# Linear attention and two MLPs on one core: PSUM tiles by bank, and loads over 128 partitions

## The chip, the cores and the metric

The kernel runs on one core of one Trainium2 chip. The metric is the device time of one execution in microseconds, taken as the median of several runs. Beside them one execution was profiled; every row below comes from that one.

## What is computed

Three stages follow one another. For B = 4 batches, H = 8 heads, S = 576 positions and D = 64 the attention is linear (no softmax), with an RMS norm per head and position; the result, 2304 rows of 512, goes through two MLPs with 2048 hidden units.

```python
kv  = np.einsum('bhsd,bhse->bhde', k, v)
out = np.einsum('bhsd,bhde->bhse', q, kv)
x   = out / sqrt(mean(out * out, -1) + 1e-6) * g_norm
x   = x.transpose(0, 2, 1, 3).reshape(2304, 512)
h = x @ w_in;  g = maximum(h, 0) + log1p(exp(-abs(h)));  y = g @ w_out      # first MLP
h = y @ w_in2; g = maximum(0.01 * h, h);                 return g @ w_out2  # second MLP
```

## The kernel before, in words

**Order of work.** The kernel does not issue its instructions in the order in which it names them. Every step is registered with `op` (L41): a cost for each engine that could do it (PE is TensorE, D VectorE, A ScalarE, P GpSimd, S a DMA from SyncE's queue, N nothing), a function that issues it, and keys that it reads and writes. `Plan.run` (L73) then lays all of them out greedily by due time, as its own costs see it, and issues each on the engine that it chose. Keys for PSUM are banks, `("ps", 0)` to `("ps", 7)`: two steps on different banks are independent for the planner. The waits that end up in the program are made later, by the framework, from the tiles that each instruction touches.

**PSUM.** Eight banks of 512 words per partition are allocated as four tiles of two banks, `pw[0]` to `pw[3]`, and every later step takes a slice of one of them:

```python
pw = ring(psum, "pw", 4, [P, 1024])
ps = [t[:, c:c + 512] for t in pw for c in (0, 512)]
```

So banks 0 and 1 are one tile, as are 2 and 3, 4 and 5, 6 and 7.

**Attention.** 16 units, each two heads of one batch. `load` (L393) brings q, k and v of a unit in three DMAs of SyncE's queue, into rings of four buffers with 96 partitions: partition p holds positions 6p to 6p+5, so one run of memory is 6 x 64 words. `T` (L405) copies q together (L374, L372 or GpSimd's L376), transposes it in six pieces (L419), forms kv of both heads in twelve matmuls with 96 rows each (L426; each shows as two in the trace) and copies both out of `pw[0]` or `pw[1]`, the latter for the first ten units alone (`U_H`). `O` (L461) multiplies q by kv into `pw[2]` (L467), copies to `xy` and squares (L485 on ScalarE, L487 on VectorE or GpSimd). After four units `norm` (L491) and `X` (L538) make and apply the norms. `xy` holds x, transposed, for all 2304 columns; within a batch column r * 96 + p is position 6p + r.

**MLPs.** 24 blocks t (two MLPs by `NG` = 4 groups of 512 hidden units by `NTP` = 3 pairs of 384 tokens) with seven Strassen products each way. Each operand is split in a high and a low part, so a product is six matmuls. `product` (L810) adds x-side products into U (bank 0 or 1, alternating with s), V (bank 2) and W (bank 3); the matmul line is L820, or L910 for the first blocks in `plain` (L897). `after` (L1116) moves them on: L1139 copies U to W on ScalarE, L1127 copies V or U to SBUF, L1134 adds them on VectorE, L835 and L841 apply the activation. `parts` (L845: L849 on ScalarE, L854 on VectorE) splits the activated blocks. `second` (L1029) multiplies by the second weight, in `piece(i, j)` (L1053):

```python
bank = (6 if i in (1, 3, 5) else 4) + (j // 2 if tokens else j)
```

In the first MLP (L1082, `tokens` false) j is 0 and 1, six matmuls of 384 columns for each of two banks; i runs 0, 5, 1, 2, 3, 4, 6. In the second MLP (L1077) j is 0, 1, 2: six matmuls of 256 columns each, the first two in one bank, the third in the bank beside it. `to_y` reads the bank and adds it to `xy` (L699 on VectorE; L693 and L694 copy where nothing has been added before); L1093 copies a bank to the other pair. Pieces are interleaved with the products of the next block, seven products and ten or eleven pieces a step s.

**Around it.** x parts are kept in DRAM and brought back (L803), weights are loaded and decoded from 64-bit floats (L572 to L626) and split (L661, L665), rows of the result are stored by L1020, 128 columns of `xy` at a time, cut where the position runs of 96 columns end.

Of the kernel before, what the change touches and what calls it, by code (L numbers as in the profile page):

```python
# [133 lines left out]
def linear_attention_two_mlps(  # L134
# [39 lines left out]
    R6 = 6  # L174
    PQ = S // R6
# [168 lines left out]
    both = mstp.tile([P, 4, 8], F32, name="both")  # L344
    nc.gpsimd.memset(ones, 0.0)
# [35 lines left out]
    def from_psum(out, in_, n, bank, writes):  # L381


        def fn(e):
            if e == "A":
                nc.scalar.activation(out, in_, AF.Copy)
            else:
                nc.vector.tensor_copy(out, in_)

        return op({"A": t_a(n), "D": t_d(n)}, fn, [], [("ps", bank), *writes])  # L390


    def load(u):  # L393
        b, hp = u // NPAIR, u % NPAIR
        hs = slice(2 * hp, 2 * hp + 2)
        for nm, src in (("q", q), ("k", k), ("v", v)):
            def fn(e, nm=nm, src=src):
                nc.sync.dma_start(
                    out=lda[nm][u % NLD],
                    in_=src[b, hs].rearrange("h (p r) d -> p h r d", r=R6),  # L400
                )

            op({"S": 0.93}, fn, (), [(nm, u % NLD)])

    def T(u):  # L405
        i = u % 2
        copy_to(
            qp[i], lda["q"][u % NLD].rearrange("p h r d -> p r h d"), R6 * P,
            [("q", u % NLD)], [("qp", i)], "AD" if u == 0 else "ADP",
        )  # L410
        t = i if u < U_H else 0
        k0, k1 = ("ps", 2 * t), ("ps", 2 * t + 1)
        qc = pw[t][:, 32:32 + S]
        kv = pw[t][:, 32 + S:32 + S + D]
        ka, va = lda["k"][u % NLD], lda["v"][u % NLD]

        def f_t(e):
            for r in range(R6):
                nc.tensor.transpose(  # L419
                    qc[:, r * PQ:(r + 1) * PQ], qp[i][:, r, :, :], ident[0:PQ, 0:PQ]  # L420
                )

        def f_kv(e):
            for r in range(R6):
                for h in range(2):
                    nc.tensor.matmul(  # L426
                        kv[h * D:(h + 1) * D, :], ka[:, h, r, :], va[:, h, r, :],
                        start=(r == 0), stop=(r == R6 - 1), tile_position=(0, h * D),
                    )

        op({"PE": 0.5}, f_t, [("qp", i)], [k0, k1])
        op({"PE": 0.75}, f_kv, [("k", u % NLD), ("v", u % NLD)], [k1])
# [24 lines left out]
    o_, s_of = pw[2][:, 0:S], pw[2][:, S:S + HS]  # L457
# [3 lines left out]
    def O(u):  # L461
        b, hp, i = u // NPAIR, u % NPAIR, u % 2
        cols = slice(b * S, (b + 1) * S)

        def f_o(e):
            for c0, c1 in ((0, 512), (512, S)):
                nc.tensor.matmul(  # L467
                    o_[:, c0:c1], kvm[i], qt[i][:, c0:c1], start=True, stop=True
                )
# [21 lines left out]
    def norm(b):  # L491
        def f_s(e):
            for w in range(NB):
                for c in range(4):
                    nc.tensor.matmul(
                        s_of[32 * c:32 * (c + 1), :], ones[:, 6 - 2 * w:38 - 2 * w],
                        sq[w][:, c * HS:(c + 1) * HS], start=(w == 0), stop=(w == NB - 1),
                        tile_position=(0, 32 * c),
                    )

        sk, rk = [("ps", 5)], [("rs", b % 2)]
# [3 lines left out]
            lambda e: nc.scalar.activation(fa, s_of, AF.Ln, bias=eps_b, scale=2.0 ** -SHIFT / D),  # L505
# [32 lines left out]
    def X(u):  # L538
# [10 lines left out]
        op({"PE": 0.28}, f_b, [("rs", b % 2), ("pick",)], RK)  # L549
# [10 lines left out]
    def decode_w(F, which, a_reg):  # L560
# [22 lines left out]
        op({"S": (1.65, 1.4)[which]}, f_l, after_loads if (which, f) < (1, GF) and which else (), rk)  # L583
# [105 lines left out]
    def to_xy(dst, src, n, first, bank, xk):  # L689
        if first:  # L690
            op(
                {"D": t_d(n), "A": t_a(n)},
                lambda e: nc.vector.tensor_copy(dst, src) if e == "D"  # L693
                else nc.scalar.activation(dst, src, AF.Copy),  # L694
                [("ps", bank)], xk,
            )
        else:
            op(
                {"D": t_d(n)}, lambda e: nc.vector.tensor_tensor(dst, src, dst, ALU.add),  # L699
                [("ps", bank)] + xk, xk,  # L700
            )
# [195 lines left out]
    def plain(s, k_):  # L897
        c = block(0, s, k_)
        w_ = wst[s % 2]
        for m in range(2):  # L900
            o = ps[2 + m][:, :BN]
            for j in range(2):
# [3 lines left out]
                def fn(e, j=j, o=o, e_=e_, W_=W_, part_=part_):  # L906
                    for kk in range(2):
                        at = part_ * 256 + kk * P
                        for n, (a, b) in enumerate(((0, 0), (0, 1), (1, 0))):
                            nc.tensor.matmul(  # L910
                                o, W_[:, a, at:at + P], e_[:, b, kk, :],
# [117 lines left out]
    def second(t):  # L1029
# [9 lines left out]
        def to_y(i, bank, j0, j1):  # L1039
            a, k_ = S_TO[i]  # L1040
            c0 = (2 * tp + k_) * BN
            if tokens:
                c0, n = c0 + j0 * P, (j1 - j0) * P
                dst = xy[:, 2 * a:2 * a + 2, c0:c0 + n].rearrange("p a (j n) -> p j a n", n=P)
                src = ps[bank][:, (j0 % 2) * 256:(j0 % 2) * 256 + 2 * n]
                src = src.rearrange("p (j a n) -> p j a n", a=2, n=P)
                kcs, n = [2 * a, 2 * a + 1], 2 * n
            else:
                kcs, n = [2 * a + j0], BN
                dst, src = xy[:, kcs[0], c0:c0 + BN], ps[bank][:, :BN]  # L1050
            to_xy(dst, src, n, g % NG == 0 and i in ((5, 1, 2, 6) if pre else (0, 1, 2, 6)), bank, xyk(kcs, c0, n // len(kcs)))

        def piece(i, j):  # L1053
# [4 lines left out]
            y = ps[bank]  # L1058
# [4 lines left out]
            def fn(e):  # L1063
                if widens:
# [23 lines left out]
            if i == 0 and pre:  # L1088
                if not tokens or j:
# [3 lines left out]
                        lambda e: nc.scalar.activation(ps[bank + 2][:, :n], y[:, :n], AF.Copy),  # L1093
# [22 lines left out]
    def after(s, i):  # L1116

        cA, cB = (block(s // 2, s % 2, k_) for k_ in range(2))
        U, V, W = (ps[u_bank(s, x_)][:, :BN] for x_ in range(3))
# [5 lines left out]
        def copy(c, m, src, bank):  # L1125
            op(
                {"A": t_a(BN)}, lambda e: nc.scalar.activation(c[:, m, :], src, AF.Copy),  # L1127
# [3 lines left out]
        def plus(c, m, src, bank):  # L1131
            op(
                {"D": t_d(BN)},
                lambda e: nc.vector.tensor_tensor(c[:, m, :], src, c[:, m, :], ALU.add),  # L1134
# [3 lines left out]
        if i == 0:  # L1138
            op({"A": t_a(BN)}, lambda e: nc.scalar.activation(W, U, AF.Copy), bu, bw)  # L1139
# [9 lines left out]
        elif i == 5:  # L1149
            act(s, lambda: cA[:, 1, :], lambda: W, BN, bw, ck(cA, 1))  # L1150
        else:
            act(s, lambda: cA[:, 0, :], lambda: U, BN, bu, ck(cA, 0))
# [5 lines left out]
    def norm_done(e):  # L1158
# [5 lines left out]
        buf(p, "lf", F32)  # L1164

# [15 lines left out]
    def warm(e):  # L1181
        for _ in range(N_WARM):
            nc.tensor.transpose(ps[7][:, 0:P], ident, ident)
# [22 lines left out]
    for i in range(NU + 1):  # L1206
        if i in W1_AT:
# [4 lines left out]
            plan.AHEAD = Plan.AHEAD  # L1212
        if i < NU:
# [16 lines left out]
       + [(t, i) for t in "qkv" for i in range(NLD)])  # L1230
    op({"N": 0.0}, norm_done, (), granules("rc", "lf")
       + [("sq", i) for i in range(NB)] + [("rs", i) for i in range(2)]
# [105 lines left out]
```

## Time and profile before

| | us |
|---|---|
| three runs | 840.98, 846.70, 846.88 (median 846.7) |
| the profiled execution | 844.57 |
| its span, first to last instruction | 842.6 |
| outside the span | 2.0 |

The span is what the trace shows; the time of an execution adds what lies around it. The attention takes the first 80 us or so, the MLPs the rest. PE's busy time counts from a matmul's start to its modelled end, and successive matmuls overlap; so the time that a row of matmuls needs is read from start to start.

### The profile page before, as it was taken

Reading aid. Unit: us, or ns where it says so; the run is one execution under the profiler, and the core shown is the slowest. Engines: PE = TensorE matmul, PEld = TensorE weight load, DVE = VectorE, ACT = ScalarE, POOL = GpSimd, SP = SyncE. Lnnn points to the kernel's source line nnn. Section 1 sums busy time; section 2 is a strip of 40 time slices with the busy share of each in tenths; the row PEclk is TensorE's granted clock in tenths of the full one; section 3 lists DMA queues with packets and bytes.
Section 4 is the critical chain, followed back from the end, with each engine's and each line's share of the span. In section 5 each row is a group of like instructions: output and inputs, shape, how many; then the busy total and the mean of one; then the engine's idle time right before and its main releaser. Section 6 shows DMA issues by size and latency. Waiting matters only on the chain. (4 is left out here: it accounts for less than half of the span.)

```text
span 842.6 us, 13729 instructions
## 1 busy us (share of the span) xinstructions
PE 796.1 (94%) x5309; PEld 750.1 (89%) x5309; DVE 677.9 (80%) x1049; ACT 537.3 (64%) x883; POOL 17.7 (2%) x26
## 2 busy tenths in 40 slices
PE   7879899999999999899999999999999999999996
PEld 6668789999899999899988988999999999999996
DVE  3787899999788987885798998898789876876565
ACT  2667878878577775764577687686577555454441
POOL 2220000000000000000000000000000000000000
PEclk9999999999999999999999999999999999999999
DMA  9995467675864884763676959674874752662814
GB/s 254 267 262 194 194 231 275 235 279 201 322 243 150 288 300 152 267 240 129 232 279 227 342 195 405 249 284 142 324 239 170 292 210 102 214 223 92 286 39 112
DMA packets 71249, 192.52 MB, mean 228 GB/s; under 512 B 5520, under 2 KB 45456, under 8 KB 71184
## 3 DMA queue, kind: packets, MB, share of 16 engines
q1 hardware_dynamic: 69504, 190.86, 64.9%
q8 instruction: 41, 0.67, 0.3%
q10 hardware_dynamic: 1680, 0.79, 0.3%
q14 instruction: 24, 0.20, 0.1%
HBM read 152.31 MB, written 39.32 MB: 227 GB/s over the span
## 5 line engine op out<-in xcount | busy, mean ns | idle before, releaser
L820 PE MATMUL pw<-ra 128*128 128x384 f32 x1932 | 390.5, 337 | 9.0 <-ACT pw L1139 3.4
L820 PEld LDWEIGHTS pw<-ra 128*128 128x128 f32 x1932 | 331.3, 188 | 16.3 <-ACT pw L1139 6.5
L1077 PE MATMUL pw<-rb 128*128 128x256 f32 x1512 | 209.6, 285 | 9.6 <-DVE xy L699 6.9
L1077 PEld LDWEIGHTS pw<-rb 128*128 128x128 f32 x1512 | 195.3, 189 | 22.6 <-DVE xy L699 17.1
L1082 PE MATMUL pw<-rb 128*128 128x384 f32 x1008 | 206.5, 339 | 7.8 <-DVE xy L699 3.7
L1082 PEld LDWEIGHTS pw<-rb 128*128 128x128 f32 x1008 | 174.6, 188 | 19.0 <-DVE xy L699 10.6
L699 DVE TENSOR_TENSOR xy<-pw,xy 128x384 f32<-128x384 f32 (+2 forms) x247 | 134.1, 549 | 71.3 <-PE pw L1077 49.9
L849 ACT ACTIVATE rb<-mf 128x768 fp32r<-128x768 f32 x154 | 129.2, 845 | 76.1 <-PE pw L1077 41.0
L854 DVE TENSOR_TENSOR rb<-mf,rb 128x768 fp32r<-128x768 f32 x154 | 146.6, 952 | 23.5 <-ACT rb L849 23.0
L1127 ACT ACTIVATE mf<-pw 128x384 f32<-128x384 f32 x92 | 44.7, 488 | 33.8 <-PE pw L820 32.9
L934 DVE TENSOR_TENSOR mf<-mf 128x768 f32<-128x768 f32 x68 | 64.1, 952 | 2.8 <-ACT mf L835 2.2
L1134 DVE TENSOR_TENSOR mf<-pw,mf 128x384 f32<-128x384 f32 x92 | 50.7, 553 | 12.8 <-PE pw L820 10.1
L1139 ACT ACTIVATE pw<-pw 128x384 f32<-128x384 f32 x46 | 22.1, 481 | 25.7 <-PE pw L820 25.3
L835 ACT ACTIVATE mf<-mf 128x768 f32<-128x768 f32 x26 | 22.0, 845 | 19.1 <-DVE mf L1134 19.0
L1093 ACT ACTIVATE pw<-pw 128x384 f32<-128x384 f32 (+2 forms) x44 | 21.1, 479 | 16.2 <-PE pw L1077 9.0
L999 DVE TENSOR_TENSOR rb<-rc,rb 128x512 fp32r<-128x512 f32 x44 | 29.7, 683 | 0.3 <-ACT rb L996 0.3
L996 ACT ACTIVATE rb<-rc 128x512 fp32r<-128x512 f32 x44 | 27.3, 626 | 2.0 <-PE pw L1077 0.8
L841 ACT ACTIVATE mf<-mf 128x768 f32<-128x768 f32 x24 | 20.2, 841 | 8.3 <-DVE mf L1134 8.2
L694 ACT ACTIVATE xy<-pw 128x384 f32<-128x384 f32 (+2 forms) x40 | 18.9, 481 | 10.3 <-PE pw L1077 4.8
L841 ACT ACTIVATE mf<-pw 128x384 f32<-128x384 f32 x32 | 15.7, 491 | 11.6 <-PE pw L820 11.2
L835 ACT ACTIVATE mf<-pw 128x384 f32<-128x384 f32 x32 | 15.6, 488 | 11.4 <-PE pw L820 11.3
L467 PE MATMUL pw<-qt,kvm 128*128 128x512 f32 (+1 forms) x64 | 20.2, 439 | 1.8 <-DVE fm L518 1.7
(116 smaller groups left out, 701.7 us busy)
## 6 DMA issues: line engine op xcount, KB each, us to landing
ra<-xscr SPq DMA_DIRECT2D x131, 768.0 KB, 6.3
xscr<-ra SPq DMA_DIRECT2D x30, 768.0 KB, 4.7
mf<-in_moe_w_in_dram SPq DMA_DIRECT2D x18, 512.0 KB, 6.1
mf<-in_moe_w_out_dram SPq DMA_DIRECT2D x18, 512.0 KB, 5.2
lf<-in_moe_w_in_dram SPq DMA_DIRECT2D x14, 512.0 KB, 6.2
lf<-in_moe_w_out_dram SPq DMA_DIRECT2D x14, 512.0 KB, 4.8
xscr<-xy SPq DMA_DIRECT2D x8, 768.0 KB, 6.2
qa<-in_q_dram SPq DMA_DIRECT2D x16, 288.0 KB, 8.7
```

Source lines behind the costliest of these rows:

```text
L699: {"D": t_d(n)}, lambda e: nc.vector.tensor_tensor(dst, src, dst, ALU.add),
L820: nc.tensor.matmul(o, w_[:, a, c:c + P], e_[:, b, kk, :], start=(not on and which < 2 and kk == 0 and n == 0), stop=(kk == 1 and n == 2), ...
L835: {"A": t_a(n)}, lambda e: nc.scalar.activation(dst(), src(), AF.Softplus),
L841: lambda e: nc.scalar.activation(dst(), src(), AF.Prelu, alpha=0.01),
L849: {"A": t_a(n)}, lambda e: nc.scalar.activation(g[:, 0, :, :], c.ap, AF.Copy),
L854: lambda e: nc.vector.tensor_tensor(g[:, 1, :, :], c.ap, g[:, 0, :, :].bitcast(F32), ALU.subtract),
L934: lambda e: nc.vector.tensor_tensor(to.ap, x.ap, y.ap, ALU.subtract),
L999: lambda e: ENG[e].tensor_tensor(w_[:, 1], src(), w_[:, 0].bitcast(F32), ALU.subtract), sk + hk, lk,
L1077: nc.tensor.matmul(y[:, 256 * (j % 2):256 * (j % 2 + 1)], G_[:, a, m, js], w_[:, b, m, :], **flags)
L1082: nc.tensor.matmul(y[:, :BN], w_[:, a, m, js], G_[:, b, m, :], **flags)
L1127: {"A": t_a(BN)}, lambda e: nc.scalar.activation(c[:, m, :], src, AF.Copy),
L1134: lambda e: nc.vector.tensor_tensor(c[:, m, :], src, c[:, m, :], ALU.add),
```

## The change

- PSUM: the two-bank tiles stay while the attention runs, in two pools (`psa` with `pw[0]`, `pw[2]`, `pw[3]`; `psb` with `pw[1]`). Before unit 10 (of 0 to 15) `psb` is closed and banks 2 and 3 come back as two tiles of one bank; when the norms are done the other six do. All uses of `ps[...]` are evaluated at issue (`src()`, `out()`), as the tiles exist only then.
- q, k, v: partition p holds positions 4p to 4p+3 of the first 512, in 128 partitions, five buffers in place of four; the last 64 positions of all heads of a batch come in one DMA per tensor and batch, in 64 partitions (runs of 64 words), with the other 64 partitions set to zero. A unit's transposes are five of 128 columns, its kv ten matmuls with 128 rows.
- Squares go to ScalarE or VectorE; GpSimd keeps the copies of q.
- In batches 1 and 3 the last 64 positions come first among the columns of `xy`, so a store of 128 columns meets one run, or two of 64 between two batches.
- Some costs that the planner uses change (loads of q, k, v and of weights, transposes, kv, `X`).

```diff
-        rows = out[b * S:(b + 1) * S, :].rearrange("(p r) d -> r p d", r=R6)
-        runs += [(PQ, rows[r]) for r in range(R6)]
+        rows = out[b * S:b * S + 4 * P, :].rearrange("(p r) d -> r p d", r=4)
+        left = (RL, out[b * S + 4 * P:(b + 1) * S, :])
+        runs += [left] * (b % 2) + [(P, rows[r]) for r in range(4)] + [left] * (1 - b % 2)
...
-    psum = ctx.enter_context(tc.tile_pool(name="psum", bufs=1, space=PSUM))
-    pw = ring(psum, "pw", 4, [P, 1024])
-    ps = [t[:, c:c + 512] for t in pw for c in (0, 512)]
+    psa = tc.tile_pool(name="psa", bufs=1, space=PSUM, side="right")
+    psb = tc.tile_pool(name="psb", bufs=1, space=PSUM)
+    psap, psbp = psa.__enter__(), psb.__enter__()
+    pw = [(psbp if i == 1 else psap).tile([P, 1024], F32, name=f"pw{i}") for i in range(4)]
+    ps = [None] * 8
+
+    def banks(old, name, which, **kw):
+        old.__exit__(None, None, None)
+        p = ctx.enter_context(
+            tc.tile_pool(name=name, bufs=1, space=PSUM, reuse_waits="tile", **kw)
+        )
+        for i in which:
+            ps[i] = p.tile([P, 512], F32, name=f"ps{i}")
...
-    NLD = 4
+    NLD = 5
-    lda = {nm: ring(attp, nm + "a", NLD, [PQ, 2, R6, D]) for nm in "qkv"}
-    qp = ring(attp, "qp", 2, [PQ, R6, 2, D])
+    lda = {nm: ring(attp, nm + "a", NLD, [P, 2, 4, D]) for nm in "qkv"}
+    ldr = {nm: ring(attp, nm + "r", 2, [P, H, D]) for nm in "qkv"}
+    qp = ring(attp, "qp", 2, [P, 4, 2, D])
+    for t, e_ in enumerate((nc.vector, nc.gpsimd)):
+        for n in "qkv":
+            e_.memset(ldr[n][t][RL:], 0.0)
...
-                    in_=src[b, hs].rearrange("h (p r) d -> p h r d", r=R6),
+                    in_=src[b, hs, 0:4 * P, :].rearrange("h (p r) d -> p h r d", r=4),
+        if hp == 0:
+            for nm, src in (("q", q), ("k", k), ("v", v)):
+                def fn(e, nm=nm, src=src):
+                    nc.sync.dma_start(
+                        out=ldr[nm][b % 2][:RL], in_=src[b, :, 4 * P:S, :].rearrange("h p d -> p h d")
+                    )
...
-            for r in range(R6):
-                nc.tensor.transpose(
-                    qc[:, r * PQ:(r + 1) * PQ], qp[i][:, r, :, :], ident[0:PQ, 0:PQ]
-                )
+            for r in range(4):
+                nc.tensor.transpose(qc[:, r * P:(r + 1) * P], qp[i][:, r, :, :], ident)
+
+        def f_tl(e):
+            nc.tensor.transpose(pw[t][:, 4 * P:5 * P], ql[:, h2, :], ident)
...
-            for r in range(R6):
+            for r in range(5):
...
-        op({"A": t_a(S), "D": t_d(S), "P": t_p(S)}, f_s, xk, [("sq", u % NB)])
+        op({"A": t_a(S), "D": t_d(S), }, f_s, xk, [("sq", u % NB)])
...
+        banks(psa, "psc", (0, 1, 4, 5, 6, 7), side="right")
...
+        if i == U_H:
+            op({"N": 0.0}, lambda e: banks(psb, "psd", (2, 3)), (), [("ps", 2), ("ps", 3)])
```

## Rows read from the trace of the kernel before

**Rows 1.** The page's first part: busy time, share of the span, instructions.

```profile
PE 796.1 (94%) x5309; PEld 750.1 (89%) x5309; DVE 677.9 (80%) x1049; ACT 537.3 (64%) x883; POOL 17.7 (2%) x26
```

**Rows 2.** Busy time by stretch; last three columns: granted clock, DMA share, GB/s.

```profile
10.00:30.00 20.00, 15.97 (x227) 11.65 (x226) 9.28 (x21) 9.07 (x18) 2.57 (x4) 1.00 1.09 271
30.00:50.00 20.00, 15.96 (x199) 12.13 (x198) 15.76 (x28) 13.74 (x27) 6.58 (x7) 1.00 1.09 262
...
200.00:300.00 100.00, 96.76 (x545) 93.65 (x544) 87.47 (x138) 69.24 (x112) 0.00 (x0) 1.00 0.65 234
300.00:400.00 100.00, 97.19 (x543) 93.28 (x541) 77.74 (x119) 59.96 (x96) 0.00 (x0) 1.00 0.60 219
400.00:500.00 100.00, 95.91 (x564) 91.34 (x564) 89.43 (x129) 71.36 (x116) 0.00 (x0) 1.00 0.71 253
...
700.00:800.00 100.00, 97.62 (x672) 93.56 (x671) 69.43 (x106) 48.75 (x78) 0.00 (x0) 1.00 0.53 182
```

**Rows 3.** PE's matmuls from 92 us on: busy us, mean ns, idle before.

```profile
L820 PE MATMUL pw<-ra 128*128 128x384 f32 x1932 | 390.5, 337 | 9.0 <-ACT pw L1139 3.4 <-DVE mf L1134 1.8 <-ACT mf L835 1.4
L1077 PE MATMUL pw<-rb 128*128 128x256 f32 x1512 | 209.6, 285 | 9.6 <-DVE xy L699 6.9 <-ACT xy L694 1.4 <-ACT pw L1093 0.3
L1082 PE MATMUL pw<-rb 128*128 128x384 f32 x1008 | 206.5, 339 | 7.8 <-DVE xy L699 3.7 <-ACT xy L694 1.9 <-DVE xy L693 1.1
L910 PE MATMUL pw<-ra 128*128 128x384 f32 x9 | 1.9, 334 | 0.0
```

**Rows 4.** The chain that ended last: start, us, what.

```profile
596.06 1.44 PE pw L1077 x12
597.49 1.04 PE pw L820 x6
```

**Rows 5.** Waits of PE's weight loads from 92 us: total, times, longest.

```profile
PEld pw L1077 <- DVE xy L699: 17.1, 31, 1.1
PEld pw L1082 <- DVE xy L699: 10.6, 24, 1.7
PEld pw L820 <- ACT pw L1139: 6.5, 11, 1.1
...
PEld pw L1082 <- DVE rb L854: 1.4, 2, 1.1
...
PEld pw L1082 <- ACT pw L1093: 0.2, 1, 0.2
```

**Rows 6.** Timeline in the first MLP: start, us, engine, what, [idle before].

```profile
302.19 1.20 PE L1082 MATMUL pw<-rb 128*128 128x384 f32 x6
...
304.10 0.55 DVE L699 TENSOR_TENSOR xy<-pw,xy 128x384 f32<-128x384 f32 x1
...
304.70 1.01 PEld L1082 LDWEIGHTS pw<-rb 128*128 128x128 f32 x6 [0.59 <-DVE xy L699]
304.70 1.33 PE L1082 MATMUL pw<-rb 128*128 128x384 f32 x6 [0.27 <-DVE xy L699]
```

**Rows 7.** Timeline in the second MLP and at its end.

```profile
810.95 0.68 DVE L699 TENSOR_TENSOR xy<-pw,xy 128x512 f32<-128x512 f32 x1
...
811.68 1.69 PE L1077 MATMUL pw<-rb 128*128 128x256 f32 x12
...
837.30 0.98 PE L1077 MATMUL pw<-rb 128*128 128x256 f32 x6 [0.52 <-DVE xy L699]
```

**Rows 8.** DMA traffic from 10 to 60 us, in 40 slices.

```profile
GB/s 281 277 278 278 286 280 273 263 279 252 253 265 261 277 243 284 242 275 275 278 270 272 274 263 280 250 259 262 244 272 238 235 270 268 270 269 272 275 272 263
```

**Rows 9.** DMA traffic from 300 to 400 us, in 40 slices.

```profile
GB/s 101 402 339 334 418 414 417 386 30 0 7 0 29 329 270 317 282 397 417 406 179 8 202 0 3 37 320 253 320 380 424 433 245 7 0 0 0 42 337 283
```

**Rows 10.** Groups of instructions of the attention, first 80 us.

```profile
L426 PE MATMUL pw<-va,ka 96*64 96x64 f32 x384 | 14.7, 225 | 6.5 <-DMA va<-in_v_dram 6.5
...
L419 PE MATMUL pw<-ident,qp 96*128 96x96 f32 x96 | 11.1, 252 | 3.6 <-POOL qp L376 3.1 <-DVE qp L374 0.3 <-ACT qp L372 0.3
...
L487 POOL TENSOR_TENSOR sq<-xy 128x576 f32<-128x576 f32 x5 | 6.0, 1193 | 8.5 <-DVE xy L477 6.3 <-ACT xy L475 2.2
```

More of the change, by code (lines that the diff above doesn't have):

```diff
@@ L173, in linear_attention_two_mlps @@
     NF = DFF // P
-    R6 = 6
-    PQ = S // R6
+    RL = S - 4 * P
     NPAIR = H // 2
@@ L399, in fn @@
                     out=lda[nm][u % NLD],
-                    in_=src[b, hs].rearrange("h (p r) d -> p h r d", r=R6),
+                    in_=src[b, hs, 0:4 * P, :].rearrange("h (p r) d -> p h r d", r=4),
                 )
-            op({"S": 0.93}, fn, (), [(nm, u % NLD)])
+            first = "qkv".index(nm) - 60.0 if u == 0 else None
+            op({"S": 0.74}, fn, (), [(nm, u % NLD)], due=first)
+        if hp == 0:
[4 more added lines that the diff above has]
+                    )
+                op({"S": 0.6}, fn, (), [(nm + "r", b % 2)])
     def T(u):
-        i = u % 2
+        b, hp, i = u // NPAIR, u % NPAIR, u % 2
+        h2 = slice(2 * hp, 2 * hp + 2)
         copy_to(
-            qp[i], lda["q"][u % NLD].rearrange("p h r d -> p r h d"), R6 * P,
+            qp[i], lda["q"][u % NLD].rearrange("p h r d -> p r h d"), 4 * P,
             [("q", u % NLD)], [("qp", i)], "AD" if u == 0 else "ADP",
@@ L455, in T, with o_of, s_of @@
         op({"A": t_a(S), "D": t_d(S)}, f_c, [], [k0, k1, ("qt", i)])
-    o_, s_of = pw[2][:, 0:S], pw[2][:, S:S + HS]
+    def o_of(b):
+        return pw[2][:, 4 * P - RL:] if b % 2 else pw[2][:, 0:S]
+    def s_of(b):
+        return pw[2][:, 0:HS] if b % 2 else pw[2][:, S:S + HS]
     r_ = pw[3][:, 512 - 2 * HS:512 - 2 * HS + S]
@@ L463, in O @@
         cols = slice(b * S, (b + 1) * S)
+        o_ = o_of(b)
         def f_o(e):
[L466 to L469, printed above, removed]
+            at = b % 2 * RL
+            nc.tensor.matmul(
+                o_[:, at:at + 4 * P], kvm[i], qt[i][:, 0:4 * P], start=True, stop=True
+            )
+            at = (1 - b % 2) * 4 * P
+            nc.tensor.matmul(
+                o_[:, at:at + RL], kvm[i], qt[i][:, 4 * P:S], start=True, stop=True
+            )
         op({"PE": 0.98}, f_o, [("kvm", i), ("qt", i)], OK)
@@ L495, in f_s @@
                     nc.tensor.matmul(
-                        s_of[32 * c:32 * (c + 1), :], ones[:, 6 - 2 * w:38 - 2 * w],
+                        s_[32 * c:32 * (c + 1), :], ones[:, 6 - 2 * w:38 - 2 * w],
                         sq[w][:, c * HS:(c + 1) * HS], start=(w == 0), stop=(w == NB - 1),
@@ L581, in decode_w @@
         rk, ak = r.keys(), a_reg.keys()
-        op({"S": (1.65, 1.4)[which]}, f_l, after_loads if (which, f) < (1, GF) and which else (), rk)
+        op({"S": (1.47, 1.3)[which]}, f_l, after_loads if (which, f) < (1, GF) and which else (), rk)
         op(
@@ L900, in plain, with o @@
         for m in range(2):
-            o = ps[2 + m][:, :BN]
+            def o(m=m):
+                return ps[2 + m][:, :BN]
             for j in range(2):
@@ L1044, in to_y, with src @@
                 dst = xy[:, 2 * a:2 * a + 2, c0:c0 + n].rearrange("p a (j n) -> p j a n", n=P)
-                src = ps[bank][:, (j0 % 2) * 256:(j0 % 2) * 256 + 2 * n]
-                src = src.rearrange("p (j a n) -> p j a n", a=2, n=P)
+                def src():
+                    y = ps[bank][:, (j0 % 2) * 256:(j0 % 2) * 256 + (j1 - j0) * 256]
+                    return y.rearrange("p (j a n) -> p j a n", a=2, n=P)
                 kcs, n = [2 * a, 2 * a + 1], 2 * n
@@ L1049, in to_y @@
                 kcs, n = [2 * a + j0], BN
-                dst, src = xy[:, kcs[0], c0:c0 + BN], ps[bank][:, :BN]
+                dst, src = xy[:, kcs[0], c0:c0 + BN], lambda: ps[bank][:, :BN]
             to_xy(dst, src, n, g % NG == 0 and i in ((5, 1, 2, 6) if pre else (0, 1, 2, 6)), bank, xyk(kcs, c0, n // len(kcs)))
@@ L1063, in fn @@
             def fn(e):
+                y = ps[bank]
                 if widens:
@@ L1092, in piece @@
                         {"A": t_a(n)},
-                        lambda e: nc.scalar.activation(ps[bank + 2][:, :n], y[:, :n], AF.Copy),
+                        lambda e: nc.scalar.activation(
+                            ps[bank + 2][:, :n], ps[bank][:, :n], AF.Copy
+                        ),
                         [("ps", bank)], [("ps", bank + 2)],
@@ L1118, in after @@
         cA, cB = (block(s // 2, s % 2, k_) for k_ in range(2))
-        U, V, W = (ps[u_bank(s, x_)][:, :BN] for x_ in range(3))
+        U, V, W = (lambda x_=x_: ps[u_bank(s, x_)][:, :BN] for x_ in range(3))
         bu, bv, bw = ([("ps", u_bank(s, x_))] for x_ in range(3))
@@ L1149, in after @@
         elif i == 5:
[L1150 removed]
+            act(s, lambda: cA[:, 1, :], W, BN, bw, ck(cA, 1))
         else:
[L1152 removed]
+            act(s, lambda: cA[:, 0, :], U, BN, bu, ck(cA, 0))
     def attention_done(e):
@@ L1229, in linear_attention_two_mlps @@
        + [(t, i) for t in ("qp", "qt", "kvm") for i in range(2)]
-       + [(t, i) for t in "qkv" for i in range(NLD)])
+       + [(t, i) for t in "qkv" for i in range(NLD)]
+       + [(t + "r", i) for t in "qkv" for i in range(2)])
     op({"N": 0.0}, norm_done, (), granules("rc", "lf")
+       + [("ps", i) for i in (0, 1, 4, 5, 6, 7)]
        + [("sq", i) for i in range(NB)] + [("rs", i) for i in range(2)]
```

49 lines of the change are left out of this document (28 added, 21 removed).

## The prediction

> **What bounds the kernel now.** I read the page's busy shares first. PE is busy 796.1 of 842.6 us and VectorE 677.9; GpSimd does next to nothing [rows 1]. So the question is where PE idles. The stretches show two regimes [rows 2]. From 10 to 30 us, PE is busy 15.97 of 20 us and the DMA engines are at 1.09 of their share, with 271 GB/s: the attention is fed by saturated queues. From 200 us on PE has 96 to 98 of 100 us, DMA 0.53 to 0.71, and VectorE between 69.4 (700 to 800) and 89.4 us (400 to 500). [...]
>
> Busy time flatters PE, since matmuls overlap. From start to start, six matmuls of 384 columns take 1.04 us and twelve of 256 take 1.44 [rows 4], that is 173.3 and 120 ns each. From 92 us on there are 1932 + 1008 + 9 of the first kind and 1512 of the second [rows 3]: 511.2 + 181.4 = 692.6 us. The last group starts at 837.30 and lasts 0.98 [rows 7], so the MLP stage takes 838.3 - 92 = 746.3 us. **53.7 us of it are not matmuls.**
>
> How much of that is waiting? PE's rows give 9.0 + 9.6 + 7.8 = 26.4 us of idle time [rows 3], the weight loads' rows 55.0 us in all (18 rows, the largest two, two others and the last shown) [rows 5]. One stall shows how these relate [rows 6]: the group at 302.19 and the product after it need 2 x 1.04 us, so the next group was due at 304.27 and came at 304.70. It lost 0.43 us, where PE's row says 0.27 and the weight loads' row 0.59: the mean of both. By the mean of both sums, waits cost 41 us; the other 13 us are 3 ns or so per matmul.
>
> Nearly all those waits are for an instruction that reads or writes PSUM: L699, L1139 and the like; the clear exceptions, such as L854, have 1.4 us and less a row [rows 5].
>
> **What those waits are for.** In the first MLP two L1082 groups in a row are j = 0 and j = 1, in different banks by the code. The L699 at 304.10 reads what the group of 302.19 wrote; it ends at 304.65, and the next group, for the bank beside it, starts 0.05 us later [rows 6]. It had no business with that bank. In the second MLP the twelve matmuls at 811.68 begin with j = 2, whose bank is not the one that a 512-word read (j = 0 and 1) takes; they start 0.05 us after that read's end at 811.63 [rows 7]. L820's wait for L1139 is the same: a copy into W (bank 3) holds up a product into V (bank 2). So I read the waits as made per tile, and the tile has two banks. The planner, whose keys are banks, had put the next group there because it thought it free.
>
> **The change part by part.**
>
> *One-bank tiles in the MLPs.* What ends later once the neighbour's wait is gone? PE's next piece needs its own bank, last read one group further back; with a product between, that is 0.72 + 1.04 to 2 x 1.04 us of grace, as much as the longest wait of the main rows (1.7) [rows 5]. [...] VectorE has 10.6 us to spare in 400 to 500 and 12.5 in 200 to 300 [rows 2], more than PE's some 5.5 us of stalls per 100 us (41 / 7.46), so it is no bound by itself, but a dense stretch can still be late. Of 41 us, 2.7 are waits on data that stay (L854's and three smaller rows of that answer); of the 38 left I count on 24, near two thirds. The ends: a third (13) if late reads only move the stall by a group, 36 if almost everything goes. Allocating the tiles costs no instruction. The hand-over waits for the last reader of the old tile, which the banks' keys asked for before.
>
> *Loads of q, k, v.* Before: 16 x 3 x 294,912 bytes = 14.16 MB, at the 270 GB/s of the stretch from 10 to 60 us [rows 8] 52.4 us of queue time. After: 12.58 MB in runs of 1024 bytes over 128 partitions, and 12 DMAs with 6144 runs of 256 bytes, 1.57 MB. Neither form stands in the trace alone. Traffic of whole 128-partition tiles reaches 402 to 433 GB/s at its best and 270 to 330 in the slices around 337 us [rows 9], so the main part lies between 12.58 / 0.414 = 30.4 and, at today's rate, 46.6 us; I take 300 GB/s, the lower group, as the runs get shorter than now: 41.9. The remainders lie between 3.8 us (414 GB/s) and 34.9 us, if a run of 256 bytes holds an engine as long as one of 1536 does now (1536 x 16 / 270 GB/s = 91 ns; 6144 x 91 / 16). I take half of today's rate, 11.6 us, nearer the lower end as bytes shrink six-fold. Sum 53.5 against 52.4: +1 us, with ends at -18 and +29. The twelve extra issues on SyncE's queue come where the queue waits on the engines anyway.
>
> [...]
>
> *PE's share of the attention.* The kv matmuls go from 24 records a unit to 20: 14.7 us x 4 / 24 = 2.4 us less [rows 10]. Transposes go from six of 96 columns to five of 128 (576 to 640 columns): 11.1 us busy before, between 9 and 12 after; I take no change. Little of the 2.4 counts while the queues lead; after 70 us no kv matmul is left to save on. I take -2 with the shorter copies of q (512 words a unit in place of 768).
>
> *Squares off GpSimd.* Five of 1.19 us [rows 10] become five of some 0.7 us on ScalarE or VectorE, both under half busy at 10 to 30 us and at 0.69 and 0.79 at 30 to 50 [rows 2]: hidden; uncovered they would be 3.6 us. Memsets of the zero halves lie under the first loads.
>
> *Stores.* 20 pieces in place of 36, under matmuls but for the last ones; nothing, at most 0.5 us at the end.
>
> **Sum.** Against the profiled execution, 844.6 us (2.0 outside the span): -24 + 1 - 2 = -25, so **820 us**. The median of the runs, 846.7, lies 2 us above the profiled execution; the range takes that in.
>
> **The rivals.**
>
> *VectorE is late next.* PE's stalls move from "the neighbour's read" to "my own bank's read". For it: 87 to 89 us of 100 busy in two stretches. Against: 69.4 and 77.7 in two others, and the waits are short against the grace. The gain is the lower end, 13, with -1 from the attention less 2 for the extra squares: 834.
>
> *The remainders hold the queues* (the slower side). Each 256-byte run costs an engine what a long run costs, 91 ns, and the attention, bound by its queues, grows by 29 us: 844.6 - 24 - 2 + 29 = 848. It ends above today from 83 ns a run on. For it: the queues are saturated from 10 to 60 us [rows 8], so nothing hides it. Against: a sixth of the bytes.
>
> *The loads get fast.* 128 partitions bring the rate of the other tiles, 414 GB/s, and the remainders half of it, 7.6 us: 38 in place of 52.4. PE then takes over as the attention's bound (it idles 4 of 20 us at 10 to 30 [rows 2]), so at most 10 us count: 844.6 - 24 - 10 = 810. [...]
>
> *The change does not do it.* The waits are not per tile: PE waits for VectorE's place in its queue, and the neighbour's read is only the last thing passed. Then the stage keeps its 746 us and the time is 844. Against: the 0.05 us after the neighbour's read, in both MLPs [rows 6, 7].
>
> **How the numbers follow.** 820 has 0.64, with 806 to 832 as its own range; VectorE late, 834, has 0.13; fast loads, 810, 0.10; no effect, 844, 0.07; slow remainders, 848, 0.06. The range that holds 8 in 10 goes from 804 (24 to 30 saved in the MLPs and 10 in the attention) to 837. A measurement tells about 1% from no change, 8.4 us. Faster by more: 820 and 810 whole, most of 834, together 0.84; within: the rest of 834, no effect and half of the slow remainders, 0.12; slower 0.04.
>
> **What would show it.** Right: PE's weight loads' waits for L699 and L1139 fall from 17.1 + 10.6 + 6.5 us to a third or less; the groups of L1082 follow each other at 1.04 us though the read of the group before is still running; the stage from the first L820 to the last L1077 falls from 746 to about 722 us; the first L820 still comes at 90 to 92 us. Wrong: the waits stay with the same names, or the same time turns up as L699 waiting while VectorE is full; or the first L820 comes at 100 us and later with 4 us waits for q, and the DMA share stays over 1 beyond 70 us.

## The result, and the profile after

The changed kernel takes 782.13 us (median of four runs, 781.27 to 782.43), the kernel before 845.62 beside it (840.98 to 846.88): a ratio of 0.926, with a 95% interval from 0.922 to 0.929. The prediction of 820 us had the right sign, and both the time and its range (804 to 837) were too high: 63 us went where 25 were counted.

First the page of the profile after, its first part, which answers to [rows 1]; then the stretches, which answer to [rows 2] (last three columns: granted clock, DMA share, GB/s).

```profile
PE 767.9 (98%) x5229; PEld 751.8 (96%) x5229; DVE 677.3 (87%) x1050; ACT 536.3 (69%) x888; POOL 13.0 (2%) x26
```

```profile
10.00:30.00 20.00, 17.99 (x216) 12.56 (x212) 9.39 (x22) 11.40 (x22) 2.12 (x3) 1.00 1.04 315
30.00:50.00 20.00, 17.90 (x190) 13.13 (x190) 18.21 (x32) 17.65 (x34) 4.04 (x5) 1.00 1.07 312
200.00:300.00 100.00, 100.00 (x578) 100.00 (x578) 88.44 (x140) 70.91 (x117) 0.00 (x0) 1.00 0.71 265
300.00:400.00 100.00, 100.00 (x579) 100.00 (x578) 84.43 (x130) 62.39 (x100) 0.00 (x0) 1.00 0.60 216
400.00:500.00 100.00, 99.81 (x659) 99.41 (x658) 95.95 (x142) 82.23 (x137) 0.00 (x0) 1.00 0.88 334
```

PE has no idle time left from 200 to 400 us, and 0.2 us of it in the densest stretch, 400 to 500 us, where VectorE is at 95.95 of 100. VectorE does the same work as before (677.3 and 677.9 us) in a shorter span. In the attention the queues are still full from 10 to 50 us (DMA share, the mean busy share of the 16 DMA engines, is over 1), but they move 315 and 312 GB/s instead of 271 and 262.

PE's groups from the first product on, by the new line numbers (L864 is the old L820, L1126 the old L1077, L1131 the old L1082), answer to [rows 3]; the two waits of the weight loads that are long enough to be listed from 80 us on answer to [rows 5].

```profile
L864 PE MATMUL ps<-ra 128*128 128x384 f32 x1932 | 386.4, 335 | 0.2 <-DMA ra<-xscr 0.2
L1126 PE MATMUL ps<-rb 128*128 128x256 f32 x1512 | 204.1, 282 | 0.0
L1131 PE MATMUL ps<-rb 128*128 128x384 f32 x1008 | 201.5, 334 | 0.2 <-DVE rb L898 0.2
```

```profile
PEld ps L1131 <- DVE rb L898: 0.5, 1, 0.5
PEld ps L864 <- ACT ps L1142: 0.5, 1, 0.5
```

Not one wait for a reader of the neighbouring bank is left, where two lines alone had 17.1 and 10.6 us: the first is for data (`rb`), and for the second PE's own row of L864, above, names a reload of x parts (`ra<-xscr`); the named L1142 had ended 0.5 us before. Matmul groups now follow each other at 1.04 us. The last line is the read, by ScalarE, of the bank that the group of 85.97 wrote (j = 0). It starts after the group of 88.05 has begun in the bank beside it (j = 1), which no longer waits for it:

```profile
84.93 1.20 PE L864 MATMUL ps<-ra 128*128 128x384 f32 x6
85.97 1.20 PE L1131 MATMUL ps<-rb 128*128 128x384 f32 x6
87.01 1.20 PE L864 MATMUL ps<-ra 128*128 128x384 f32 x6
88.05 1.20 PE L1131 MATMUL ps<-rb 128*128 128x384 f32 x6
...
88.19 0.47 ACT L738 ACTIVATE xy<-ps 128x384 f32<-128x384 f32 x1
```

Where the 62.5 us of span went, by the starts and ends of PE's groups in the two traces:

| us | before | after | difference |
|---|---|---|---|
| span's start to first product | 92.33 | 84.93 | -7.40 |
| first product to last matmul of the MLPs | 745.95 | 691.76 | -54.19 |
| last matmul to span's end | 4.3 | 3.4 | -0.9 |

One microsecond stands in the wrong line: before, six matmuls of the first blocks came behind the first product (6 x 0.173 us); after, all 96 come ahead of it. So the MLP stage gave 53.2 us and the attention 8.4. The stage after is its matmuls summed as in the prediction, 2940 x 0.1733 + 1512 x 0.12 = 691.0 us, plus 0.7.

### The profile page after: what moved, and what is told of

Read it like the earlier page. It is cut to its first block, busy times and chain, and to the rows that moved or that the text cites. A ratio compares the mean times of both kernels' runs of the same rounds, so it can differ in the third digit from the quotient of the medians.

```text
span 780.1 us, 13522 instructions
## 1 busy us (share of the span) xinstructions
PE 767.9 (98%) x5229; PEld 751.8 (96%) x5229; DVE 677.3 (87%) x1050; ACT 536.3 (69%) x888; POOL 13.0 (2%) x26
## 4 chain that ended last, share of the span: by engine, by line
PE 90%; DVE 5%; DMA 2%; SPq 1%; ACT 1%; issue 1%; POOL 0%; DVEq 0%; ACTq 0%
PE ps L864 41%; PE ps L1126 23%; PE ps L1131 21%; PE pw L505 1%; DMA qa<-in_q_dram 1%; PE pw L454 1%; DMA va<-in_v_dram 1%; DMA ra<-xscr 1%; PE ps L956 1%; DVE ra L766 1%; DVE rb L898 1%; SPq L412 1%; DVE rb L1045 1%; PE pw L588 1%; PE pw L443 1%
## 5 line engine op out<-in xcount | busy, mean ns | idle before, releaser
L864 PE MATMUL ps<-ra 128*128 128x384 f32 x1932 | 386.4, 335 | 0.2 <-DMA ra<-xscr 0.2
L864 PEld LDWEIGHTS ps<-ra 128*128 128x128 f32 x1932 | 331.9, 188 | 0.6 <-ACT ps L1142 0.5
L1126 PE MATMUL ps<-rb 128*128 128x256 f32 x1512 | 204.1, 282 | 0.0
L1131 PE MATMUL ps<-rb 128*128 128x384 f32 x1008 | 201.5, 334 | 0.2 <-DVE rb L898 0.2
L1126 PEld LDWEIGHTS ps<-rb 128*128 128x128 f32 x1512 | 198.2, 189 | 0.1
L1131 PEld LDWEIGHTS ps<-rb 128*128 128x128 f32 x1008 | 177.0, 188 | 0.5 <-DVE rb L898 0.5
L898 DVE TENSOR_TENSOR rb<-mf,rb 128x768 fp32r<-128x768 f32 x154 | 146.6, 952 | 23.8 <-ACT rb L893 22.5
L743 DVE TENSOR_TENSOR xy<-ps,xy 128x384 f32<-128x384 f32 (+2 forms) x247 | 134.6, 548 | 33.3 <-PE ps L1126 21.8
L1178 ACT ACTIVATE mf<-ps 128x384 f32<-128x384 f32 x92 | 44.6, 487 | 27.2 <-PE ps L864 26.4
L1185 DVE TENSOR_TENSOR mf<-ps,mf 128x384 f32<-128x384 f32 x92 | 50.6, 553 | 10.9 <-PE ps L864 9.4
L1190 ACT ACTIVATE ps<-ps 128x384 f32<-128x384 f32 x46 | 22.0, 479 | 24.6 <-PE ps L864 24.1
L879 ACT ACTIVATE mf<-mf 128x768 f32<-128x768 f32 x26 | 21.9, 843 | 15.1 <-DVE mf L1185 14.9
L1142 ACT ACTIVATE ps<-ps 128x384 f32<-128x384 f32 (+2 forms) x44 | 21.1, 481 | 7.2 <-PE ps L1131 3.7
L885 ACT ACTIVATE mf<-ps 128x384 f32<-128x384 f32 x32 | 15.7, 489 | 9.1 <-PE ps L864 8.9
L738 ACT ACTIVATE xy<-ps 128x384 f32<-128x384 f32 (+2 forms) x37 | 17.7, 484 | 5.7 <-PE ps L1126 2.7
```

The source lines that it names most:

```text
L743: {"D": t_d(n)}, lambda e: nc.vector.tensor_tensor(dst, src(), dst, ALU.add),
L864: nc.tensor.matmul(o, w_[:, a, c:c + P], e_[:, b, kk, :], start=(not on and which < 2 and kk == 0 and n == 0), stop=(kk == 1 and n == 2), ...
L885: lambda e: nc.scalar.activation(dst(), src(), AF.Prelu, alpha=0.01),
L898: lambda e: nc.vector.tensor_tensor(g[:, 1, :, :], c.ap, g[:, 0, :, :].bitcast(F32), ALU.subtract),
L1126: nc.tensor.matmul(y[:, 256 * (j % 2):256 * (j % 2 + 1)], G_[:, a, m, js], w_[:, b, m, :], **flags)
L1131: nc.tensor.matmul(y[:, :BN], w_[:, a, m, js], G_[:, b, m, :], **flags)
```

## The experiments

Two theories stood against each other at the start. A: the whole gain is the waits for the neighbouring bank, and the loads and the rest are small. B: another part of the change, or the new order of steps that the planner finds with it, freed PE. Each kernel was compared with the kernel before on the same chip.

**The kernel before with one-bank tiles alone.** The kernel before, with the change's PSUM allocation and nothing else (shown is the allocation; the uses of `ps[...]` are evaluated at issue, as in the change):

```
-    pw = ring(psum, "pw", 4, [P, 1024])
-    ps = [t[:, c:c + 512] for t in pw for c in (0, 512)]
+    pw = [(psbp if i == 1 else psap).tile([P, 1024], F32, name=f"pw{i}") for i in range(4)]
+    ps = [None] * 8
...
+            ps[i] = p.tile([P, 512], F32, name=f"ps{i}")
```

> The kernel before with one-bank PSUM tiles in the MLPs and nothing else of the change. Theory A (waits made for a two-bank tile cost the whole 53 us that the MLP stage lost): the stage takes some 692 us, the time is 844.6 - 53 - 1 = 790 us (786 to 794), and the first L820 still comes at 92 us. Rival B (the stage is free of stalls because the planner, with the new loads and costs, puts the steps in another order): the stage keeps some 745 us and the time stays at 835 to 845 us.

It took 790.44 us against 842.70, a ratio of 0.939 (0.936 to 0.941): 52 of the 63 us. The MLP stage went from 745.95 to 695.32 us. The first product came at 86.05 us, sooner than the 92 expected: the first blocks' waits in the attention went too (shown with the pairs below), and its loads, though unchanged, ran at 286 GB/s from 10 to 60 us where the first profile of before has 267. All waits of its weight loads that are listed from the first product (86.05 us) on, with times and the longest, and then PE's own row of the products:

```profile
PEld ps L1097 <- DVE rb L864: 1.6, 2, 1.1
PEld ps L830 <- DVE ra L732: 1.2, 1, 1.2
PEld ps L830 <- ACT mf L1144: 0.8, 1, 0.8
```

```profile
L830 PE MATMUL ps<-ra 128*128 128x384 f32 x1932 | 386.5, 335 | 1.5 <-DVE ra L732 0.9 <-DMA ra<-xscr 0.6
```

The first two are waits for data (`rb`, `ra`), as the prediction had them stay. The third is put down to L1144, which had ended 0.5 us before; PE's own row has a reload of x parts (`ra<-xscr`) in its place. None is for a reader of PSUM's neighbour.

**The change with two-bank tiles kept.** The changed kernel, allocating its banks in pairs in the MLPs too:

```
-            ps[i] = p.tile([P, 512], F32, name=f"ps{i}")
+            if i // 2 in (0, 1, 2, 3):
+                if i % 2 == 0:
+                    w = p.tile([P, 1024], F32, name=f"pd{i}")
+                    ps[i], ps[i + 1] = w[:, 0:512], w[:, 512:1024]
+            else:
+                ps[i] = p.tile([P, 512], F32, name=f"ps{i}")
```

> The kernel after, but the six and two banks come back as tiles of two banks each, sliced as before; the order of the steps is that of the kernel after. Theory A: the stalls of the MLP stage return, 782 + 53 = 835 us (831 to 838), and only the 8 us by which the first product came earlier remain. Rival B: the time stays at 782 to 788 us.

833.69 us, ratio 0.990 (0.988 to 0.992). The planner's keys are banks in either form, so the order of the work is that of the changed kernel; the waits are back, in nearly the old amounts (waits of its weight loads from the first product on; L1131, L1136 and L869 are the second MLP, the first, and the product):

```profile
PEld pd L1131 <- DVE xy L748: 17.1, 30, 1.5
PEld pd L1136 <- DVE xy L748: 10.6, 25, 1.7
PEld pd L869 <- ACT pd L1195: 6.4, 9, 1.2
```

So theory A holds in the main: the granularity of the tile is worth 52 us by either route, and the rest of the change 9 (842.70 less 833.69). In the profiles, 50.6 and 47.6 us of it lie in the MLP stage.

**Pairs for half of the banks.** In the first of these two the condition of the edit above takes banks 0 to 3 (the products' U, V and W), in the second banks 4 to 7 (the second multiplication):

```
+            if i // 2 in (0, 1):
...
+            if i // 2 in (2, 3):
```

> The kernel after with banks 0 and 1, and 2 and 3, as tiles of two banks (U, V, W of the products) and single tiles for 4 to 7. By the weight loads' waits before (14 of 53 us for L820, 39 for L1077 and L1082) theory A has 782 + 14 = 796 us (792 to 800). If the two kinds of stall cover for each other, less: under 790 us. Rival B: 782 us.

> The kernel after with banks 4 and 5, and 6 and 7, as tiles of two banks (the second weight's products) and single tiles for 0 to 3. Theory A: 782 + 39 = 821 us (815 to 825). Rival B: 782 us.

801.98 us (ratio 0.952, 0.949 to 0.955) and 819.27 (0.972, 0.969 to 0.976): 20 and 37 us over the changed kernel, expected 14 and 39; the first lies outside its expected 792 to 800. Their largest waits, the first kernel's line and then the second's two:

```profile
PEld pd L869 <- ACT pd L1195: 9.5, 13, 1.4
```

```profile
PEld pd L1131 <- DVE xy L748: 16.4, 31, 1.1
PEld pd L1136 <- DVE xy L748: 12.5, 28, 1.7
```

What the first had beyond the expectation is in the attention: its MLP stage is 16.9 us longer than the changed kernel's, and its first product comes 4.2 us later, at 89.15. The first blocks use banks 2 and 3 while the attention runs, and their weight loads' waits are back with those banks in pairs and not with the others (up to 92 us, first kernel, then second):

```profile
L961 PEld LDWEIGHTS pd<-ra 128*128 128x128 f32 x96 | 16.3, 188 | 4.2 <-ACT mf L405 3.0 <-DVE mf L407 1.0 <-issue 0.2
```

```profile
L961 PEld LDWEIGHTS ps<-ra 128*128 128x128 f32 x96 | 16.4, 188 | 0.3 <-issue 0.2
```

In the MLP stages 16.9 + 34.8 is 4 more than the 47.6 of both together. I read this as one stall giving the readers at the other place time to finish; no run shows it apart. Most of the price lies at the second multiplication, where VectorE's read (L748 here, L743 in the changed kernel) is what is waited for.

**Both kernels once more, on one chip.** For the spread of the attention between executions.

> The kernel before once more, profiled on the chip of the three runs beside it, since its DMA rate in the attention may differ from chip to chip: 10 to 50 us at 262 to 291 GB/s, the first L820 at 86 to 93 us, the MLP stage with 50 to 55 us of waits, 841 to 847 us.

> The kernel after on the same chip: 779 to 783 us. Both theories of the attention's 8 us meet here: if the loads make it, the DMA rate from 10 to 50 us is over 300 GB/s and above that of the kernel before on this chip by a sixth; if the one-bank tiles make it (banks 2 and 3, free for the first blocks), the rates are alike and PE's waits for L386 are what is gone.

The kernel before took 840.13 us in one run, the changed one 783.37, with a ratio of 0.926 (0.923 to 0.930) to all runs of before on that chip. The MLP stage of before was 744.54 us (745.95 in the first profile), that of after 693.27 (691.76). Most of the difference is in the attention: DMA traffic from 10 to 60 us in the first profile of before, and in this one:

```profile
DMA packets 10156, 13.35 MB, mean 267 GB/s; under 512 B 832, under 2 KB 10150, under 8 KB 10150
```

```profile
DMA packets 10721, 14.48 MB, mean 290 GB/s; under 512 B 878, under 2 KB 10587, under 8 KB 10714
```

With it the first product came at 89.15 us instead of 92.33. So the prediction's "today's rate" was one of several. From 10 to 50 us the changed kernel moved 329 and 325 GB/s (two stretches of 20 us) on this chip, where the kernel before moved 296 and 285: an eighth more, where the expectation had a sixth. The waits for L386, 1.5 us of PE's idle time before, are gone too. So both of the expectation's theories have a part in the attention's gain.

**Squares allowed on GpSimd again.** The changed kernel, with the old choice of engines:

```
-        op({"A": t_a(S), "D": t_d(S), }, f_s, xk, [("sq", u % NB)])
+        op({"A": t_a(S), "D": t_d(S), "P": t_p(S)}, f_s, xk, [("sq", u % NB)])
```

> The kernel after, with the squares allowed on GpSimd again. Prediction's view (the squares' move is hidden): within 1 us of the kernel after. Rival (GpSimd's tensor_tensor slows VectorE's instructions beside it, L617 at 0.98 us in place of 0.46): 1 to 3 us slower than the kernel after.

783.77 us (ratio 0.927, 0.924 to 0.931), beside the changed kernel's 783.37 on that chip. GpSimd took six squares, in 6.9 us, and nothing came of it in the total: this edit is hidden, as predicted. The planner laid the steps out anew, though (first product at 80.23 us with 84 of the 96 first-block matmuls done), so the two kernels differ in more than one engine's work.

**The remainder loads twice, into the same tile.** Meant as the price of the short runs in the queues:

```
+                    for _ in range(2):
                         nc.sync.dma_start(
                             out=ldr[nm][b % 2][:RL], in_=src[b, :, 4 * P:S, :].rearrange("h p d -> p h d")
                         )
```

> The kernel after, with each of the 12 loads of the last 64 positions issued twice, to the same place: 6144 more runs of 256 bytes. By the prediction's middle value (half of the old rate) they cost 11.6 us of queue time, by its lower bound 3.8, by its upper 34.9. While the queues bound the attention, the kernel gets slower by about that: 794, 786 or 817 us. If the queues no longer bound it, under 3 us.

820.97 us, 38 over the changed kernel and beyond all three expected values, but not for the queues' rate. The waits of SyncE's queue (SPq) up to 100 us, two issues from its timeline, and the stretch from 10 to 30 us:

```profile
SPq L423 <- DMA qr<-in_q_dram: 20.6, 4, 6.6
SPq L423 <- DMA kr<-in_k_dram: 13.4, 4, 4.1
SPq L423 <- DMA vr<-in_v_dram: 9.5, 4, 2.5
```

```profile
19.07 6.76 SPq L423 DMA_DIRECT2D qr<-in_q_dram  x2
25.88 0.62 SPq L412 DMA_DIRECT2D ka<-in_k_dram  x1
```

```profile
10.00:30.00 20.00, 10.55 (x95) 7.11 (x94) 4.24 (x8) 4.52 (x8) 1.24 (x2) 0.74 0.64 184
```

The second load waits until the first has landed, and the next load (L412) is issued only behind it, 6.8 us after the pair began. Meanwhile the DMA share is 0.64, PE is busy 10.55 of 20 us, and its granted clock has a mean of 0.74; the changed kernel has 1.04, 17.99 us and 1.00 there. Of the price of short runs this says nothing; it shows what 43.5 us of waits at the head of that queue cost, together with the lower clock that came with them.

**Four buffers, and the remainders beside them.** To repeat the measurement without that wait, the second load goes to a tile of its own that nothing reads; its memory is taken from the ring, so the first of these kernels has the smaller ring alone:

```
-    NLD = 5
+    NLD = 4
...
+    ldx = {nm: ring(attp, nm + "x", 1, [P, H, D]) * 2 for nm in "qkv"}
...
-                    nc.sync.dma_start(
-                        out=ldr[nm][b % 2][:RL], in_=src[b, :, 4 * P:S, :].rearrange("h p d -> p h d")
-                    )
+                    for to in (ldr, ldx):
+                        nc.sync.dma_start(
+                            out=to[nm][b % 2][:RL], in_=src[b, :, 4 * P:S, :].rearrange("h p d -> p h d")
+                        )
```

> The kernel after with four buffers in place of five for q, k and v each; it is here to stand beside the next kernel. If the queues bound the attention, as in the prediction, a fifth buffer lets them run further ahead without making them faster: within 2 us of the kernel after (782), first product at 84 to 86 us. Rival (the fifth buffer gives the attention's gain): first product 3 to 6 us later, 785 to 788.

> The kernel with four buffers, and each of the 12 remainder loads (6144 runs of 256 bytes in all) issued a second time, into a tile of its own that nothing reads. Measures the price of the remainders in the queues, where the prediction had 11.6 us between 3.8 and 34.9. If the queues bound the attention and short runs cost half of today's rate: 8 to 14 us over the four-buffer kernel (790 to 798). If a short run holds an engine as long as a long one: 25 to 35 us (807 to 820). If the queues have room by now or short runs go at full rate: under 4 us (782 to 788).

782.02 us (ratio 0.927, 0.925 to 0.929) and 794.78 (0.942, 0.940 to 0.944). The fifth buffer is worth nothing. The second set of remainders costs 12.8 us, all of it in the attention: the first product comes at 96.97 us in place of 84.29. The stretch from 50 to 70 us, of four buffers and then with the remainders beside them:

```profile
50.00:70.00 20.00, 19.34 (x223) 15.69 (x223) 18.02 (x34) 16.09 (x32) 2.32 (x2) 1.00 0.73 263
```

```profile
50.00:70.00 20.00, 16.60 (x176) 12.21 (x174) 14.98 (x28) 14.11 (x28) 3.55 (x4) 0.96 0.97 275
```

The queues stay full (DMA share 0.97) where they had emptied (0.73). By the DMAs' landings it is queue time: the last load of q, k and v lands at 68.47 us in place of 55.78, 12.7 us later too. 1.57 MB in 12.7 us is 124 GB/s, about half of the 267 of before, and the prediction had 11.6 us.

**More work for VectorE.** How far was VectorE from being late? The first kernel moves the copy of U into W to it, the second also the copies into the blocks:

```
-            op({"A": t_a(BN)}, lambda e: nc.scalar.activation(W(), U(), AF.Copy), bu, bw)
+            op({"D": t_d(BN)}, lambda e: nc.vector.tensor_copy(W(), U()), bu, bw)
...
-                {"A": t_a(BN)}, lambda e: nc.scalar.activation(c[:, m, :], src(), AF.Copy),
+                {"D": t_d(BN)}, lambda e: nc.vector.tensor_copy(c[:, m, :], src()),
```

> The kernel after with the copy of U into W (L1190, one per product step, 45 of 0.48 us on ScalarE) on VectorE instead: some 45 x 0.55 = 25 us more work on VectorE, 677 to 702 of 780 us. Theory (VectorE had slack, so that PE's waits go wholly): at most 3 us slower, 782 to 786, weight loads' waits under 5 us. Rival (VectorE was just short of being the bound): 10 to 20 us slower, and the weight loads wait for VectorE's reads.

> As the kernel before this one, and the copies of V and U into the blocks (L1178, 90 of 0.49 us on ScalarE) go to VectorE too: some 50 us more, 677 to 752 of 780 us, 96% of the span. Theory: here VectorE is late next, as the prediction's rival had it for the change itself: 15 to 45 us slower than after, 797 to 827, with weight loads waiting for VectorE's reads. Rival (VectorE's lateness never decides while its sum is below the span): under 6 us slower.

787.07 us (784.30 to 787.73; ratio 0.932, 0.930 to 0.935) and 795.96 (0.943, 0.940 to 0.946). The first is 5 us over the changed kernel, more than the 3 of the theory and less than the rival's 10; the second is 14 over, just under the 15 to 45 expected. In the first's profiled run, the fastest, it is 2.2 us. VectorE's busy time went to 695.3 and 728.8 us, by 18 and 51 us, less than the 25.8 and 76.6 us of the copies (the planner shifted other work to ScalarE). Two stretches of the second kernel, from 200 to 300 and from 400 to 500 us, its largest waits, and PE's row of the products:

```profile
200.00:300.00 100.00, 100.00 (x579) 100.00 (x578) 96.63 (x158) 63.97 (x96) 0.00 (x0) 1.00 0.69 261
400.00:500.00 100.00, 92.48 (x569) 88.69 (x568) 93.74 (x141) 67.52 (x106) 0.00 (x0) 0.98 0.79 285
```

```profile
PEld ps L864 <- DVE mf L1185: 3.1, 2, 2.8
PEld ps L1131 <- issue: 2.2, 2, 1.9
PEld ps L1131 <- DVE rb L898: 2.0, 4, 1.3
```

```profile
L864 PE MATMUL ps<-ra 128*128 128x384 f32 x1932 | 388.2, 336 | 5.9 <-DMA ra<-xscr 4.2 <-DVE mf L1178 1.5
```

Here VectorE is late: PE idles 7.5 us from 400 to 500, and the weight loads' waits name L1185 and L898 ("issue" is time for which the profile shows no wait). Not all of it is named: PE's product groups put 4.2 us of their 5.9 down to reloads of x parts (`ra`), and what made those late was not followed. With 51 us more work the stage loses 16.7 us over pure matmuls, with 18 more 3.0, and 0.7 as it is. So VectorE was near the edge, but on the good side of it. Its busy share doesn't tell where the edge is: at 96.63 from 200 to 300 us PE lost nothing, at 93.74 from 400 to 500 it did.

## Why the prediction was wrong, step by step

**The waits were sized too small: the step "it lost 0.43 us ... the mean of both", and from it 41 us.** The step stopped one group too early. The stalled group of [rows 6] is followed by this one in PE's timeline of the kernel before:

```profile
305.88 1.20 PE L820 MATMUL pw<-ra 128*128 128x384 f32 x6
```

It comes 1.18 us after the stalled group's start at 304.70, not 1.04: the stalled group itself lasts 1.33 us, not 1.20. The loss is 0.43 + 0.14 = 0.57 us, which is the weight loads' 0.59 and not the mean. Over the whole stage the same holds, within 2.6 us, in every kernel of this table: loss (the stage less 173.3 ns and 120 ns for each matmul in it) beside the sums of the weight loads' waits and of PE's idle time from the first product on (those above 0.15 us).

| kernel | loss, us | weight loads' waits, us | PE's idle time, us |
|---|---|---|---|
| before | 53.9 | 54.8 | 24.5 |
| two-bank tiles kept | 48.3 | 48.7 | 21.3 |
| pairs in banks 4 to 7 | 35.6 | 37.6 | 13.5 |
| pairs in banks 0 to 3 | 17.7 | 15.1 | 8.4 |
| before with one-bank tiles | 3.2 | 3.6 | 2.5 |
| after | 0.7 | 1.0 | 0.4 |

In the four kernels with pairs PE's idle time is less than half of the loss: successive records overlap (a group of six lasts 1.20 us, and the next starts 1.04 after it), which hides part of a stall (0.27 of 0.43 us were booked above), and the longer run of a stalled group (1.33 us) is booked as busy. So the prediction's "13 us are 3 ns or so per matmul" were waits too. After, the same matmuls show 14.6 us less busy time: 806.6 us in [rows 3], 792.0 after.

**The recovery was sized too small: "of the 38 left I count on 24".** All came back, even more than the end of 36, because the 38 were some 52. The reason given for two thirds, that VectorE gets late in a dense stretch, did not come true: at 95.95 of 100 us VectorE still had the banks read in time. That each bank has two groups of grace was the right argument and should have had the weight; the discount was taken from VectorE's busy share, and the kernel with the most work on VectorE shows that this share doesn't tell (96.63 without a loss, 93.74 with one).

**The loads: "+1 us", made of 41.9 and 11.6.** The remainders were near, 12.7 measured; as 11.6 was a choice between bounds of 3.8 and 34.9, part of that is luck. The main part was not: at the 316 GB/s of the changed kernel's stretch from 10 to 60 us, the 14.16 MB take 44.8 us, so the main part took some 32, near the prediction's fast end of 30.4. This is an estimate from measured numbers; the main part was not timed alone. The sum of both can be read from the landings: the last load of q, k and v landed at 65.5, 61.5 and 61.1 us in the three profiles with the old loads (the third is the kernel before with one-bank tiles), and at 54.1 to 56.8 in the five profiles of the change and of its forms with pairs. So the loads ended some 4 to 11 us sooner, where the prediction had them 1 us longer. The traffic in 40 slices, which answers to [rows 8], has 26 slices at 300 GB/s and more, up to 395, where the highest there was 286:

```profile
GB/s 321 356 370 323 330 279 233 304 367 319 231 374 301 277 350 308 290 313 223 247 374 379 383 383 364 324 318 368 277 225 249 273 261 315 325 331 298 283 393 395
```

What made the main part faster, no run here shows: the length of the runs changed with the partitions.

**The attention: "the first L820 still comes at 90 to 92 us".** It came at 84.93 us with all first blocks done, 8.4 us sooner by that count. Two things were left out. The first blocks use banks 2 and 3 while the attention still runs, and had the same waits, before 92 us, where the prediction did not look; pairs in banks 0 to 3 brought them back, as shown above. Their weight loads up to 92 us, before and then after:

```profile
L910 PEld LDWEIGHTS pw<-ra 128*128 128x128 f32 x90 | 15.2, 188 | 2.4 <-ACT mf L386 2.2 <-issue 0.2
```

```profile
L956 PEld LDWEIGHTS ps<-ra 128*128 128x128 f32 x96 | 16.3, 188 | 0.3 <-issue 0.2
```

And the loads gained, as said. Counting the first product's time less 0.173 us for each first-block matmul done by then, before has 76.7 us (73.6 in the other execution), the two-bank form of the change 71.1, before with one-bank tiles 70.4, and after 68.3 (67.3). The loads and the rest are thus worth 2.5 to 5.6 us beside two-bank tiles and 2.1 to 3.1 beside one-bank tiles. How these few microseconds divide between the queues, PE's shorter share and the copies of q was not tried.

**The small terms.** Squares off GpSimd: hidden, as said. Stores: the tail fell from 4.3 to 3.4 us, where at most 0.5 was allowed. The change's end, as it stands now, is a read of 256 columns and the last store's issue:

```profile
776.72 0.42 DVE L743 TENSOR_TENSOR xy<-ps,xy 128x256 f32<-128x256 f32 x1 [0.35 <-PE ps L1126]
777.18 0.38 ACTq L1066 DMA_DIRECT2D out_dram<-xy  x1
```

**The rivals.** "The change does not do it" fell with the pairs kept: same planner, same order, the waits back at once. "VectorE is late next" (834, though its own terms, 844.6 - 13 - 1 + 2, give 833) did not happen, but had its place: it takes 51 us more work for 14 us. "The remainders hold the queues" fell: 12.7 us of queue time, not 34.9. "The loads get fast" (810) was partly so. What was right is the mechanism, argued from the 0.05 us after a neighbour's read: the framework waits per tile, the planner plans per bank, and one tile a bank makes them agree.

## What to carry to other kernels

Size PE's stalls by the waits of its weight loads, from the first to the last group of the stage, and check it on one stall by following it until the groups are regular again; PE's own idle row showed less than half. Where a planner or a programmer thinks in banks, allocate tiles of one bank: a tile of two makes each bank's writer wait for the neighbour's reader, at 52 us here for a matter of allocation. And look for the mechanism in every stage where it can act, not only in the one with the long rows.

## What the runs showed that was not expected

- A stalled group of six matmuls loses time twice: before it starts (0.43 us) and again inside, 1.33 us for 1.20.
- The same loads of the same kernel ran at 267 GB/s in one execution and at 290 in another, both with full queues (DMA share 1.08 to 1.09 from 10 to 50 us), and moved the attention's end by 3 us.
- A second load into a tile whose first load is still on its way held SyncE's whole queue: 43.5 us of waits, and from 10 to 30 us a DMA share of 0.64 and a mean granted clock of 0.74.
